# State-space scan and bilinear feed-forward: C of the later blocks loaded by head pairs and turned by VectorE

## The chip, the core and the metric

One NeuronCore of a Trainium2 chip runs the whole program. The metric is the device time of one execution in microseconds (us); the time before is the median of three runs. TensorE (PE) does the matrix products, its weight loads are listed as PEld; VectorE (DVE), ScalarE (ACT) and GpSimd (POOL) do elementwise work; SyncE (SP) issues most DMAs, GpSimd and ScalarE some.

## What is computed

Two stages. The first is a chunked linear recurrence over 4 x 8 sequences (batch x heads) of 768 tokens, with a state of 16 x 32 per sequence; the second is a feed-forward layer `(x Wa) * (x Wb) Wo` over the 3072 tokens, with 256 inputs and 1536 hidden columns. Cut to what matters:

```python
for c in range(nc):                       # chunks of 32 tokens
    L = np.exp(cum[..., :, None] - cum[..., None, :]) * causal
    CB = np.einsum('bhin,bhjn->bhij', Cc, Bc)
    y_intra = np.einsum('bhij,bhjd->bhid', CB * L, xc)
    y_inter = np.einsum('bhin,bhnd->bhid', Cc, state) * np.exp(cum)[..., None]
    y[:, :, sl] = y_intra + y_inter
    Bx = np.einsum('bhjn,bhjd->bhjnd', Bc, xc) * decay_from_j[..., None, None]
    state = decay_full[..., None, None] * state + np.sum(Bx, axis=2)
x = y.transpose(0, 2, 1, 3).reshape(3072, 256)
out = ((x @ w_a) * (x @ w_b)) @ w_out
```

## The kernel before

**Tiling.** The scan runs in 6 blocks of 128 tokens (not 32). A block of one pair of batches is a unit of work called a pair: pair p is block p // 2 and batches 2 (p % 2) and the next, so there are 12 pairs, two to a block. The decay factors are multiplied into B and C beforehand: C by the running product of `a` over its value in the middle of the block, B by the reciprocal of that (`fCl`, `fBl` for pairs 4 to 11; `late_rows`, `late_factors` and `fb` make them, on GpSimd and VectorE).

**One pair of 4 to 11**, step by step:
1. `loads_bc`, `loads_x`: SP issues the DMAs of C, B and x (tokens on the partitions; each run of 16 floats of B or C is 64 bytes).
2. `prep`: GpSimd scales C and B to f16, one 128x256 instruction each (`scale_bc`, L316), and x (`scale_x`, L305).
3. `transposes`: TensorE turns two 128x128 tiles of B and two of C, against the identity (L342), into a bank of PSUM; ScalarE copies B out twice, masked by the parity of the head (L346), and C once (L355).
4. `scores` (L372): 16 small products C B^T into four PSUM banks `SC`.
5. `mask`: the causal mask on the four fourths of the scores. VectorE does a fourth in one instruction (L426). Of pairs 4 to 8 the last fourth goes to GpSimd instead: ScalarE copies it out of PSUM (L423), GpSimd multiplies (L424).
6. Per block, `group`: `outputs` (L522 state part, L432 scores times x, L461 the sums for the next state), the evacuation to `XB` (ScalarE L555, VectorE L557), and on VectorE the state sums (L579).

**The feed-forward** of block k follows: 12 units (`bunit`, L693: two products into PSUM banks of the first and of the second weight matrix; ScalarE copies the first out, L639; VectorE multiplies, L703), then four output tiles (`bout`, L718), copied out by ScalarE (L730) and stored by SP (L731). For pairs 0 to 3 the units are per pair (`unit`, L615, L639, L646; `out_half`, L661, L673).

**Order.** The schedule is written out by hand: each engine takes its instructions in program order, and so does each DMA queue. What waits, holds up what stands behind it on its engine. Four PSUM banks (`ff0` to `ff3`) rotate for units, output tiles and transposes, in the order that the digits of `BANKS` give. Around the change, TensorE's order is: `group(2)`, transposes of pair 6, an output half, transposes of pair 7, another output half, scores of pair 6, units; the same with `group(3)` and pairs 8 and 9; from there on, pair by pair.

**Queues.** At the start GpSimd's queue loads the weights `Wa`, `Wb`, `Wo`, pair 1's and pair 2's inputs. SP loads pair 0's and, after the first half of `Wo` has landed, pair 3's (L851, L854, L855), then pairs 4, 5 and so on. Stores of outputs stand behind all of these loads on SP.

Of the kernel before, what the change touches and what calls it, by code (L numbers as in the profile page):

```python
# [10 lines left out]
f32 = mybir.dt.float32  # L11
# [8 lines left out]
YS = 16.0  # L20

BANKS = (
    "1301302130213023120312031023120312031203210230123012302103210320132013210231023103201231"
    "0231023102301320132013201321032103210321032103210321032130213021302130213021302130213021"
    "3021302"
)


# [1 line left out]
def kernel(  # L30
# [13 lines left out]
    nc = tc.nc  # L44
# [44 lines left out]
    Wo = big.tile([128, NK, d_model], f16, name="Wo")  # L89
    X2T = big.tile([128, P0, 2, 2, Q], f16, name="X2T")  # L90
    XB = big.tile([128, NBLK - P0 // NBP, 2, 2, NBP, Q], f16, name="XB")
    U32 = big.tile([128, NP, 2, 2 * D], f32, name="U32")
    gU = big.tile([128, NP, 2, 2 * D], f32, name="gU")
    maskbd = big.tile([128, H, D], f16, name="maskbd")
    warm = big.tile([128, 128], f16, name="warm")
    causal_q = big.tile([128, Q], f16, name="causal_q")
# [8 lines left out]
    Ps = big.tile([BH, NL, Q], f32, name="Ps")  # L105
    fBl = big.tile([128, NL, NBP * 2 * H], f32, name="fBl")
    fCl = big.tile([128, NL, NBP * 2 * H], f32, name="fCl")
    hr = big.tile([BH, NG], f32, name="hr")
    hs = big.tile([BH, NG], f32, name="hs")
    hsx = big.tile([128, nb, NG], f32, name="hsx")  # L110
# [22 lines left out]
    def bank(name):  # L133
        return psf.tile([128, 512], f32, name=name, tag=f"ff{next(banks)}")


    def tiles(p):
        Bn = inp.tile([128, H, 2, N], f32, name="bn", tag="bn")
        Cn = inp.tile([128, H, 2, N], f32, name="cn", tag="cn")
        Xn = inp.tile([128, H, 2, D], f32, name="xn", tag="xn")  # L140
        pair_in[p] = (Bn, Cn, Xn)

# [16 lines left out]
    def load2(eng, p, which):  # L159
        if p < P0:  # L160
            return [load1(eng, p, which, bt) for bt in range(2)]
        blk, bp = divmod(p, NBP)
        return eng.dma_start(
            by_token(pair_in[p][which]).rearrange("p t h n -> p (t h) n"),
            (B, C, x)[which][2 * bp : 2 * bp + 2, :, blk * Q : (blk + 1) * Q, :].rearrange("t h q n -> q (t h) n"),
        )

    def load_w(W, t, f=None):
        src = (moe_w_a if W is Wa else moe_w_b).rearrange("(f p) e -> p f e", p=128)[:, :, t * KC : (t + 1) * KC]
# [30 lines left out]
    nc.vector.memset(hsx, 0.0)  # L200
    nc.vector.memset(causal_q, 1.0)
    nc.vector.memset(c32, 0.0)
    x1 = load1(nc.sync, 1, 2, 0)
    nc.sync.dma_start(c32[0:BH], p32_t.ap())
    nc.gpsimd.affine_select(
# [70 lines left out]
    def late_rows(eng):  # L276
        k0 = P0 // NBP
        eng.tensor_tensor(
            out=Ps, in0=Pr[:, k0:], in1=rmid[:, k0:].unsqueeze(2).broadcast_to((BH, NL, Q)), op=ALU.mult
        )  # L280

    def late_factors():
        for c0 in range(0, Q, 32):
            nc.vector.transpose(fCl[c0 : c0 + 32], Ps[:, :, c0 : c0 + 32])

    st = {}
    stores = []
# [19 lines left out]
    def scale_bc(p, which, eng, factor=None):  # L307
        blk, bp = divmod(p, NBP)
        name = ("bm", "cm")[which]
        if p >= P0:  # L310
            f = (fBl, fCl)[which][:, blk - P0 // NBP].rearrange("p (b t h) -> p b t h", b=NBP, t=2)[:, bp]
        else:
            f = (f_c(blk) if which else fB[:, blk])[:, :, bp]
        raw = by_token(pair_in[p][which]) if p >= P0 else pair_in[p][which].rearrange("p h r n -> p r h n")
        m_ = pre.tile([128, 2, H, N], f16, name=name, tag=name)
        eng.tensor_tensor(  # L316
            out=m_,
            in0=raw,
            in1=(f if factor is None else factor).unsqueeze(3).broadcast_to((128, 2, H, N)),
            op=ALU.mult,  # L320
        )
        st.setdefault(p, {})[name] = m_
    def transposes(p, ps=None, between=None, apart=False):
        s = st[p]
        if p >= P0:
            ps = [bank("tr").bitcast(f16)] * 2
            TB, TC = ps[0][:, 0:256], ps[0][:, 256:512]
            on_dve = False
        elif ps is None:
            ps = [bank("tb") if p == 1 else SC[0], SC[1]] if apart else None  # L330
            on_dve = apart
            TB, TC = (TT[:, 0:256], TT[:, 256:512]) if ps is None else [t_.bitcast(f16)[:, 0:256] for t_ in ps]
        else:
            on_dve = True
            TB, TC = [t_.bitcast(f16)[:, 0:256] for t_ in ps]
        BT = mid.tile([128, 2, 2, 2, 64], f16, name="bt", tag="bt")
        CT = mid.tile([128, 2, Q], f16, name="ct", tag="ct")
        b_ = []

        def turn(T_, src):  # L340
            for r in range(2):
                nc.tensor.transpose(T_[:, r * 128 : (r + 1) * 128], src[:, r].rearrange("p h n -> p (h n)"), ident)  # L342

        def copy_bt(e):
            o_ = BT[:, e].rearrange("p r t i -> p (r t i)")
            b_.append(nc.scalar.activation(out=o_, in_=TB, func=AF.Copy, scale=par[:, e : e + 1]))  # L346

        turn(TB, s["bm"])
        if between:
            between()  # L350
        turn(TC, s["cm"])
        copy_bt(0)
        copy_bt(1)
        if p >= P0:
            nc.scalar.copy(CT.rearrange("p t q -> p (t q)"), TC)  # L355
            s["BT"], s["CT"] = BT.rearrange("p e r t i -> p e r (t i)"), CT
            return
        c_ = (nc.vector.tensor_copy if on_dve else nc.scalar.copy)(
            CT.rearrange("p t (i r) -> p r (t i)", r=2), TC.rearrange("p (r c) -> p r c", r=2)
        )  # L360
        if apart:
            for i_ in b_:
                tc.declare_no_dep(c_.ins, i_.ins.name, reason="reads of two banks")
        s["BT"], s["CT"] = BT, CT

# [205 lines left out]
    def state_sums(p, bts=(0, 1)):  # L571
        blk, bp = divmod(p, NBP)
        for bt in bts:
            g = G[:, 2 * bp + bt, blk : blk + 1]
            ds = st[p]["DS"][bt]
            if blk == 0:
                nc.vector.tensor_scalar(U32[:, p, bt], ds, g, None, ALU.mult)
            else:
                nc.vector.scalar_tensor_tensor(  # L579
                    out=U32[:, p, bt], in0=ds, scalar=g, op0=ALU.mult, in1=gU[:, p, bt], op1=ALU.add  # L580
                )

    def state_spread(p):
# [16 lines left out]
            )  # L600
        if blk + 1 < NG:
            nc.gpsimd.tensor_tensor(
                out=gU[:, p + NBP],
                in0=U32[:, p],
                in1=G[:, 2 * bp : 2 * bp + 2, blk + 1].unsqueeze(2).broadcast_to((128, 2, 2 * D)),
                op=ALU.mult,
            )
# [125 lines left out]
    def loads_bc(p, eng=None):  # L733
        if p < NP:
            tiles(p)
            for w in (1, 0):
                load2(eng or nc.sync, p, w)

    def loads_x(p, eng=None):
        if p < NP:  # L740
# [73 lines left out]
    for w in range(2):  # L814
        for bt in range(2):
            load1(nc.gpsimd, 2, w, bt)
    wo0 = load_wo(0)
    for bt in range(2):
        load1(nc.gpsimd, 2, 2, bt)
# [61 lines left out]
        out_mm(c // 2, c % 2, o[c], range(6))  # L881
    scale_bc(3, 0, nc.gpsimd)
    scale_bc(3, 1, nc.gpsimd)
    late_rows(nc.gpsimd)
    scale_x(3, nc.gpsimd)
    pull(2)
    pv(2)
    for c in range(3):
        out_mm(c // 2, c % 2, o[c], range(6, NK))
        out_store(c // 2, c % 2, o[c])  # L890
    state_sums(2)
    h = unit(2, 0, lambda: transposes(3, apart=True))
    h()
    late_factors()
    fb(2)
    h = unit(2, 1)

    def prep(p, spread=()):
        if p < NP:
            scale_bc(p, 1, nc.gpsimd)  # L900
            scale_bc(p, 0, nc.gpsimd)
        for q in spread:
            if q // NBP < NBLK - 1:
                state_spread(q)
# [33 lines left out]
        return [lambda k=k: bunit(blk, k) for k in ks]  # L938

    scores(3)  # L940
    prep(4, (2,))
    loads_x(4, nc.sync)
    for p in range(6, NP):
        loads_bc(p)
        if p < 10:
            loads_x(p - 1, nc.sync)
    mask(product(3, 3), by_pool=True)
    mask(product(3, 0))
    h()
    for m in range(1, 3):  # L950
# [3 lines left out]
    go((2, 2), (2, 3), (2, 4))  # L954
    pull(3)
    pv(3)
    go((2, 5))
    transposes(4)
    state_sums(3)
# [23 lines left out]
    h()  # L983
    go((3, 5))
    group(2)
    transposes(6)
    out_half(3, 0)
    transposes(7)
# [7 lines left out]
    scale_x(6, nc.scalar)  # L996
    bgo(2, 3, 4)
    stage(7, True)
    fb(5)
    prep(8)  # L1000
    prep(9)
    prep_x(8)
# [2 lines left out]
        loads_x(p)  # L1005
    masked(7, (0, 1, 2), *bu(2, 5, 6, 7, 8, 9, 10, 11))
    group(3)
    transposes(8)
    bout(2, 0)
    transposes(9)  # L1010
# [6 lines left out]
    masked(8, (2,), *bu(3, 0, 1, 2, 3, 4, 5))  # L1017
    for blk in range(4, NBLK):
        pB = blk * NBP + 1
        stage(pB, False)  # L1020
        if blk + 1 < NBLK:
            transposes(pB + 1)
        if blk > 4:
            prep_x(pB)
        masked(pB, (0, 1))
        bout(blk - 2, 2)
        masked(pB, (2, 3), *bu(blk - 1, 6, 7, 8, 9))
        group(blk)
        bout(blk - 2, 3)
        bgo(blk - 1, 10, 11)  # L1030
        if blk + 1 < NBLK:
            stage(pB + 1, False, (pB - 1, pB))
            prep_x(pB + 1)
            masked(pB + 1, (0, 1))
            bout(blk - 1, 0)
            masked(pB + 1, (2,))
            transposes(pB + 2)
            bout(blk - 1, 1)
            masked(pB + 1, (3,), *bu(blk, 0, 1, 2, 3, 4, 5))
    last = NBLK - 1  # L1040
    bout(last - 1, 0)
    bout(last - 1, 1)
# [37 lines left out]
```

## Time and profile before

| | us |
|---|---|
| runs: median of 3 (lowest to highest) | 124.99 (124.78 to 125.30) |
| the profiled execution, its own time | 125.11 |
| its span, first to last instruction | 123.40 |
| TensorE busy | 117.3 |
| VectorE / ScalarE / GpSimd busy | 91.0 / 75.7 / 61.2 |

The span is what the views show; the 1.71 us beside it are the same run's start and end. Busy time of TensorE counts overlapping, pipelined instructions, so it says little about how tightly they follow; the chain of work that ended last says more. It is followed back from the last instruction: at each step to what released it, or to the instruction before it on its engine. In a row of a timeline come start, length, engine, line, operation, what it writes and reads, how often, and in brackets how long the engine had been idle and what released it. In a row of a group come the count, the busy time, the mean duration in ns and the idle time before. Busy time by stage, in us:

| stretch (us) | PE | DVE | ACT | POOL | DMA share |
|---|---|---|---|---|---|
| 13 to 24 | 10.60 | 9.02 | 7.44 | 8.26 | full |
| 24 to 31.5 | 7.50 | 4.46 | 4.66 | 6.27 | 0.77 |
| 31.5 to 39.5 | 8.00 | 6.92 | 5.70 | 4.56 | 0.94 |
| 39.5 to 51 | 11.48 | 10.06 | 8.78 | 8.04 | 0.99 |
| 51 to 63 | 11.96 | 10.80 | 8.93 | 9.78 | 0.86 |
| 63 to 78 | 15.00 | 12.71 | 11.02 | 9.20 | 0.41 |
| 78 to 96 | 18.00 | 15.48 | 10.32 | 3.73 | 0.09 |

### The profile page before, as it was taken

To read this page: it belongs to the slowest core of one execution; us is meant where nothing else is said; L and a number is where in the kernel's file an instruction comes from. 1 tells how busy PE (TensorE), PEld (TensorE's weight loads), DVE (VectorE), ACT (ScalarE), POOL (GpSimd) and SP (SyncE) were. 2 spreads that over 40 slices of the span, in tenths; PEclk is the share of its full clock that TensorE was granted. 3 is DMA by queue.
4 is the path that set the end of the run, shared out by engine and by line. 5 is a ranking of instruction groups with operands and counts; after the bars stand their busy time and mean duration, and the time that the engine had idled before them with its cause. 6 is when DMAs were issued, how large, how long until landed. Compare 5 with 4: busy or idle time off the path is not lost.

```text
span 123.4 us, 3704 instructions
## 1 busy us (share of the span) xinstructions
PE 117.3 (95%) x1456; PEld 80.0 (65%) x1456; DVE 91.0 (74%) x182; ACT 75.7 (61%) x158; POOL 61.2 (50%) x88
## 2 busy tenths in 40 slices
PE   6799799999999999999999999999999999999990
PEld 2345669889898798744477465757464775555890
DVE  3999598973995979799986988996889544747200
ACT  0447846837669866987669767457637746657220
POOL 7997989099492994097996970056000000000000
PEclk9999999999999999999999999999999999999999
DMA  3999999978899989799977601011101012010122
GB/s 66 195 155 210 185 198 204 164 137 77 89 125 115 108 111 103 91 118 93 129 271 169 204 5 45 5 43 45 43 0 43 5 43 88 0 48 0 43 85 85
DMA packets 56401, 12.15 MB, mean 99 GB/s; under 512 B 51168, under 2 KB 55936, under 8 KB 56384
## 3 DMA queue, kind: packets, MB, share of 16 engines
q1 hardware_dynamic: 51808, 7.43, 36.3%
q0 software_dynamic: 2304, 4.06, 17.4%
q10 hardware_dynamic: 2272, 0.43, 1.8%
q8 instruction: 11, 0.18, 0.6%
q14 instruction: 6, 0.05, 0.1%
HBM read 11.13 MB, written 3.15 MB: 116 GB/s over the span
## 4 chain that ended last, share of the span: by engine, by line
PE 85%; DMA 7%; DVE 5%; issue 1%; ACT 0%; DVEq 0%
PE ops L718 17%; PE aps L693 17%; PE bps L693 16%; PE ops L661 9%; PE aps L615 8%; PE bps L615 7%; DMA Wb<-in_moe_w_b_dram 5%; PE SC L372 2%; PE SC L432 2%; PE tr L342 2%; DMA a_sb<-in_a_dram 2%; DVE hk L646 1%; PE bps L628 1%; PE SC L447 1%; PE SC L522 1%; DVE fC L246 1%
## 5 line engine op out<-in xcount | busy, mean ns | idle before, releaser
L639 ACT COPY asb<-aps 128x512 f32<-128x512 f32 x72 | 41.9, 587 | 16.0 <-PE aps L693 10.4
L703 DVE TENSOR_TENSOR hkb<-bps,asb 128x512 f16<-128x512 f32 x48 | 32.3, 688 | 11.8 <-ACT asb L639 10.4
L693 PE MATMUL aps<-XB,Wa 128*128 128x512 f16 x96 | 28.6, 379 | 0.0
L693 PE MATMUL bps<-XB,Wb 128*128 128x512 f16 x96 | 28.5, 379 | 0.0
L718 PE MATMUL ops<-Wo,hkb 128*128 128x256 f16 (+1 forms) x204 | 22.8, 267 | 0.0
L718 PEld LDWEIGHTS <-hkb 128*128 128x128 f16 x204 | 18.4, 98 | 3.0
L426 DVE TENSOR_TENSOR t<-SC,causal_q 128x512 f16<-128x512 f32 x27 | 17.3, 681 | 2.2 <-PE SC L372 2.2
L646 DVE TENSOR_TENSOR hk<-bps,asb 128x512 f16<-128x512 f32 x24 | 15.6, 681 | 3.5 <-ACT asb L639 2.1
L693 PEld LDWEIGHTS <-Wb 128*128 128x128 f16 x96 | 9.9, 103 | 11.0 <-issue 0.2
L693 PEld LDWEIGHTS <-Wa 128*128 128x128 f16 x96 | 9.7, 104 | 9.2 <-issue 0.3
L730 ACT ACTIVATE osb<-ops 128x256 f32<-128x256 f32 (+1 forms) x16 | 6.0, 376 | 12.7 <-PE ops L718 12.6
L615 PE MATMUL bps<-X2T,Wb 128*128 128x256 f16 x84 | 12.6, 273 | 0.1
L615 PE MATMUL aps<-X2T,Wa 128*128 128x256 f16 x84 | 12.5, 273 | 0.2 <-DVE hk L646 0.2
L305 POOL TENSOR_SCALAR x<-xn 128x512 f16<-128x512 f32 x8 | 11.9, 1489 | 0.7
L661 PE MATMUL ops<-Wo,hk 128*128 128x256 f16 x96 | 11.7, 273 | 0.0
L661 PEld LDWEIGHTS <-hk 128*128 128x128 f16 x96 | 9.0, 98 | 1.2
L615 PEld LDWEIGHTS <-Wb 128*128 128x128 f16 x84 | 8.5, 103 | 1.1 <-issue 0.5
L615 PEld LDWEIGHTS <-Wa 128*128 128x128 f16 x84 | 8.4, 104 | 1.2 <-issue 0.5
L424 POOL TENSOR_TENSOR t<-tmp,causal_q 128x512 f16<-128x512 f32 x5 | 5.8, 1156 | 6.2 <-ACT tmp L423 6.1
L426 DVE TENSOR_TENSOR t<-SC,causal 128x512 f16<-128x512 f32 x13 | 8.2, 678 | 0.3 <-PE SC L387 0.2
L595 POOL TENSOR_TENSOR spair<-U,ch 128x128 f16<-128x128 f32 x8 | 3.1, 398 | 10.3 <-DVE U L579 10.3
L346 ACT ACTIVATE bt<-tr,ch 128x256 f16<-128x256 f16 x16 | 6.7, 472 | 0.5 <-PE tr L342 0.5
(101 smaller groups left out, 136.1 us busy)
## 6 DMA issues: line engine op xcount, KB each, us to landing
out_dram<-osb SPq DMA_DIRECT2D x23, 128.0 KB, 1.8
xn<-in_x_dram SPq DMA_DIRECT2D x5, 256.0 KB, 4.6
cn<-in_C_dram SPq DMA_DIRECT2D x8, 128.0 KB, 4.3
bn<-in_B_dram SPq DMA_DIRECT2D x8, 128.0 KB, 4.7
Wo<-in_moe_w_out_dram POOLq DMA_DIRECT2D x2, 384.0 KB, 5.9
xn<-in_x_dram POOLq DMA_DIRECT2D x3, 256.0 KB, 4.8
Wa<-in_moe_w_a_dram POOLq DMA_DIRECT2D x2, 192.0 KB, 5.5
xn<-in_x_dram SPq DMA_DIRECT2D x3, 128.0 KB, 3.5
```

Of the source, the lines that this page charges most:

```text
L305: eng.tensor_scalar(xo, xi, XS, None, ALU.mult)
L346: b_.append(nc.scalar.activation(out=o_, in_=TB, func=AF.Copy, scale=par[:, e : e + 1]))
L424: nc.gpsimd.tensor_tensor(out=o_, in0=tmp, in1=c_, op=ALU.mult)
L426: nc.vector.tensor_tensor(out=o_, in0=i_, in1=c_, op=ALU.mult)
L615: nc.tensor.matmul(ps[:, kk * 2 * Q : (kk + 1) * 2 * Q], w_up(W, k, f), X2T[:, p, :, f], start=(f == 0), stop=(f == 1), skip_group_check=True,
L639: (nc.vector.tensor_copy if on_dve else nc.scalar.copy)(asb, a_ps)
L646: nc.vector.tensor_tensor(out=s["hk"][:, 2 * k2 : 2 * k2 + 2, :].rearrange("p k q -> p (k q)"), in0=b_ps, in1=asb, op=ALU.mult)
L661: nc.tensor.matmul(o_ps[:, 0:d_model], hk[:, k, bt * Q : (bt + 1) * Q], Wo[:, k, :], start=(k == 0), stop=(k == NK - 1), skip_group_check= ...
L693: nc.tensor.matmul(t_, w_up(W, k, f), XB[:, blk - P0 // NBP, f].rearrange("p t j q -> p (t j q)"), start=(f == 0), stop=(f == 1), skip_gro ...
L703: return lambda: nc.vector.tensor_tensor(out=s["hk"][:, k], in0=ps[1], in1=asb, op=ALU.mult)
L718: nc.tensor.matmul(o_ps[:, 0:w], hk[:, k, c * Q : (c + 1) * Q], Wo[:, k, cs], start=(k == 0), stop=(k == NK - 1), skip_group_check=True,)
L730: nc.scalar.activation(out=o_sb[:, 0:w], in_=o_ps[:, 0:w], func=AF.Copy, scale=1.0 / (YS * YS))
```

## The change

C of blocks 2 to 5 (pairs 4 to 11), and B of block 5 (pairs 10 and 11), take another way to the layout with heads and state on the partitions:

- **Load.** A whole block comes at once: for each of the four head pairs m and each head e of it, one DMA into 32 partitions, four neighbouring tokens (256 bytes) to a run; 8 DMAs of 32 KB for both pairs of the block (`load_block`).
- **Factors.** They are needed in this layout: `spread_rows` copies rows of `Ps` to `Pq` in 16 DMAs on SP, `block_factors` turns `Pq` on VectorE into `fCq`; `last_factors` takes the reciprocal for B of block 5, in place of `fb(5)`. `late_rows`, which computes `Ps` on GpSimd, moves ahead of the loads of `Wo`; `late_factors` and `fb(2)` move ahead of `pv(2)`.
- **Scale and turn.** GpSimd scales the block in one 128x512 instruction (`scale_block`), VectorE turns it in 32x32 blocks in one 128x512 instruction (`turn_block`), SBUF to SBUF. The transposes on TensorE and ScalarE's copy of C go; of B of block 5 the transposes go too, and ScalarE's two masked copies read SBUF.
- **Masks.** The last fourth of pairs 9, 10 and 11 goes by ScalarE and GpSimd.

`BANKS` is written anew (two banks less are taken), the number of buffers of B, C and the states changes, and `mask(product(3, 3), by_pool=True)` moves ahead of `prep(4)`.

```diff
+    def by_block(blk, which):
+        return blk >= P0 // NBP and (which == 1 or blk == NBLK - 1)
...
+    def load_block(eng, blk, which):
+        raw = inp.tile([128, nb, 2, 4, N], f32, name="rq", tag="rq", bufs=3)
+        st[("raw", blk, which)] = raw
+        for m, e in itertools.product(range(4), range(2)):
+            eng.dma_start(
+                raw[32 * m : 32 * m + 32, :, e].rearrange("i b g n -> i b (g n)"),
+                (B, C)[which][:, 2 * m + e, blk * Q : (blk + 1) * Q, :].rearrange("b (i g) n -> i b (g n)", g=4),
+            )
+
+    def scale_block(blk, which, eng):
+        f = fCq[:, blk - P0 // NBP, :, 0 : 2 * nb] if which else fBq
+        m_ = pre.tile([128, 4, nb, 2, N], f16, name="mq", tag="mq", bufs=2)
+        eng.tensor_tensor(
+            out=m_.rearrange("p g b e n -> p (b e) g n"),
+            in0=st[("raw", blk, which)].rearrange("p b e g n -> p (b e) g n"),
+            in1=f.rearrange("p g j -> p j g").unsqueeze(3).broadcast_to((128, 2 * nb, 4, N)),
+            op=ALU.mult,
+        )
+        st[("scaled", blk, which)] = m_
+
+    def turn_block(blk, which):
+        t_ = mid.tile([128, nb, Q], f16, name="tq", tag="tq", bufs=3)
+        nc.vector.transpose(
+            t_.rearrange("p b (i g) -> p g b i", g=4),
+            st[("scaled", blk, which)].rearrange("p g b e n -> p g b (e n)"),
+        )
+        st[("turned", blk, which)] = t_
...
+    nc.vector.memset(Pq, 0.0)
...
+    def last_factors():
+        nc.vector.reciprocal(fBq, fCq[:, NL - 1, :, 0 : 2 * nb])
...
+    def spread_rows(eng):
+        for m, b in itertools.product(range(4), range(nb)):
+            eng.dma_start(Pq[32 * m + 2 * b : 32 * m + 2 * b + 2], Ps[b * H + 2 * m : b * H + 2 * m + 2])
+
+    def block_factors():
+        nc.vector.transpose(
+            fCq.rearrange("p k g j -> p (k g) j"), Pq.rearrange("p k (i g) -> p k g i", g=4)
+        )
...
         if p >= P0:
-            ps = [bank("tr").bitcast(f16)] * 2
-            TB, TC = ps[0][:, 0:256], ps[0][:, 256:512]
-            on_dve = False
+            if by_block(blk, 0):
+                TB = st[("turned", blk, 0)][:, 2 * bp : 2 * bp + 2].rearrange("p t q -> p (t q)")
+            else:
+                TB = bank("tr").bitcast(f16)[:, 0:256]
...
-        turn(TB, s["bm"])
+        if not by_block(blk, 0):
+            turn(TB, s["bm"])
...
-        turn(TC, s["cm"])
+        if p < P0:
+            turn(TC, s["cm"])
...
-            nc.scalar.copy(CT.rearrange("p t q -> p (t q)"), TC)
+            s["CT"] = st[("turned", blk, 1)][:, 2 * bp : 2 * bp + 2]
...
     for w in range(2):
         for bt in range(2):
             load1(nc.gpsimd, 2, w, bt)
+    late_rows(nc.gpsimd)
+    spread_rows(nc.sync)
     wo0 = load_wo(0)
...
-    late_rows(nc.gpsimd)
     scale_x(3, nc.gpsimd)
+    late_factors()
+    fb(2)
     pull(2)
     pv(2)
...
     state_sums(2)
+    block_factors()
     h = unit(2, 0, lambda: transposes(3, apart=True))
     h()
-    late_factors()
-    fb(2)
...
     pv(3)
+    turn_block(2, 1)
     go((2, 5))
...
     group(2)
+    turn_block(3, 1)
     transposes(6)
...
-    fb(5)
+    last_factors()
...
     group(3)
+    turn_block(4, 1)
     transposes(8)
...
     for blk in range(4, NBLK):
         pB = blk * NBP + 1
-        stage(pB, False)
-        if blk + 1 < NBLK:
-            transposes(pB + 1)
+        stage(pB, True)
...
         masked(pB, (0, 1))
+        if blk + 1 < NBLK:
+            turn_block(blk + 1, 0)
         bout(blk - 2, 2)
-        masked(pB, (2, 3), *bu(blk - 1, 6, 7, 8, 9))
+        masked(pB, (2,), *bu(blk - 1, 6, 7))
+        if blk + 1 < NBLK:
+            turn_block(blk + 1, 1)
+        bgo(blk - 1, 8, 9)
+        if blk + 1 < NBLK:
+            transposes(pB + 1)
         group(blk)
...
-            stage(pB + 1, False, (pB - 1, pB))
+            stage(pB + 1, True, (pB - 1, pB))
...
-            masked(pB + 1, (3,), *bu(blk, 0, 1, 2, 3, 4, 5))
+            bgo(blk, 0, 1, 2, 3, 4, 5)
```

## The prediction

> **What bounds the kernel now.** I read the page first: busy shares, slices, and the chain that ended last.
>
> ```profile
> span 123.4 us, 3704 instructions
> ...
> PE 117.3 (95%) x1456; PEld 80.0 (65%) x1456; DVE 91.0 (74%) x182; ACT 75.7 (61%) x158; POOL 61.2 (50%) x88
> ...
> PEclk9999999999999999999999999999999999999999
> ...
> PE 85%; DMA 7%; DVE 5%; issue 1%; ACT 0%; DVEq 0%
> ```
>
> TensorE carries 85% of the chain, at full granted clock. The other engines matter only where TensorE waits for them. Next I read the chain in order of time. From 17 us on its pieces follow each other with hardly a gap; this is the turn from block 3's scan to pair 8's scores:
>
> ```profile
> 62.96 0.56 PE SC L432 x32
> 63.64 0.33 PE tr L342 x4
> 63.97 1.31 PE ops L718 x12
> 65.50 1.31 PE ops L718 x12
> 66.81 0.33 PE SC L372 x16
> ```
>
> The first output half ends at 63.97 + 1.31 = 65.28, the second starts at 65.50; pair 9's four transposes lie between: 0.22 us, 55 ns each. A transpose lasts longer than that (the group rows give 219 to 221 ns), but four overlap and only the pitch costs chain time. So work taken off TensorE is worth its pitch, unless something else arrives later than TensorE does.
>
> Third, VectorE's timeline over the same stretch:
>
> ```profile
> 63.84 0.47 DVE L579 SCALAR_TENSOR_TENSOR U<-SC,G,gU 128x64 f32<-128x64 f32 x2 [0.21 <-PE SC L461]
> ...
> 64.33 1.39 DVE L557 TENSOR_SCALAR XB<-SC 64x512 f16<-64x512 f32 x2
> ...
> 65.75 0.47 DVE L579 SCALAR_TENSOR_TENSOR U<-SC,G,gU 128x64 f32<-128x64 f32 x2
> ...
> 67.18 1.89 DVE L426 TENSOR_TENSOR t<-SC,causal_q 128x512 f16<-128x512 f32 x3 [0.96 <-PE SC L372]
> ```
>
> VectorE works without a pause to 66.22 and idles 0.96 us until the scores come. Last, the groups by shape, the SP queue's timeline and the issue times of two stores:
>
> ```profile
> L246 DVE STREAM_TRANSPOSE fC<-Pe 32x64 f32<-32x64 f32 x4 | 0.9, 235 | 0.1
> ...
> L284 DVE STREAM_TRANSPOSE fCl<-Ps 32x128 f32<-32x128 f32 x4 | 1.2, 299 | 0.0
> ```
> ```profile
> 21.63 1.28 SPq L154 DMA_DIRECT2D bn<-in_B_dram  x2
> 22.95 1.36 SPq L154 DMA_DIRECT2D cn<-in_C_dram  x2
> 24.36 1.31 SPq L154 DMA_DIRECT2D xn<-in_x_dram  x2
> ```
> ```profile
> L731 SPq DMA_DIRECT2D out_dram<-osb x16: 332/332/333, 65.7 to 120.2; - x16
> L675 SPq DMA_DIRECT2D out_dram<-osb x8: 383/406/1278, 59.3 to 63.7; - x8
> ```
>
> Two more shapes of elements give VectorE's turn: 64 more elements cost 64 ns. And an issue on SP costs 0.33 us alone, 0.41 beside other traffic.
>
> **The change, part by part** (against the profiled execution: 125.11 us, span 123.40, 1.71 around it; the median of the runs is 124.99, 0.12 lower).
>
> TensorE transposes. Pairs 4 to 9 lose C's two, 12 in all; pairs 10 and 11 lose all four, 8 in all. 20 x 55 ns = **-1.10 us** on the chain. One page speaks of far more: the Trainium skill (TensorE: Matmul & The Clock Gate, Part 4: PE-mode transpose) gives about 275 ns for one in a kernel, 5.5 us for 20 by that; the pitch in the rows decides against it.
>
> The turns. Five of 128x512 f16. From the two rows, 299 + 384 x 1.0 = 0.69 us each. No row shows f16: two elements at a time would make it 163 + 256 = 0.42, strided writes at half rate 1.2. I take 0.69, as both rows cost one element per ns.
> Each must end before its block's scores:
> - Block 4 (pair 8). It is put behind group(3), on an engine busy to 66.22: it ends at 66.93, and scores follow some 0.05 us later (ScalarE's copy at 50.72 + 0.38 = 51.10, scores at 51.15). TensorE, 0.22 us shorter over this stretch, arrives at 66.59: a new wait of 0.40. Behind the scores stand the six units of block 3.
> - Block 3 (pair 6), the same place: VectorE's sums end at 50.64, the turn at 51.35, scores at 51.41, TensorE there at 51.22 - 0.22 = 51.00: 0.41. Behind it the reciprocal fb(4) (0.35) still fits before the masks.
> - Block 2 (pair 4): VectorE is idle 0.82 us before 37.97, scores come at 39.46: nothing.
> - Block 5, C and B: between pair 9's masks and units. VectorE is behind TensorE there; with 2 x 0.69 added and one mask (0.68) gone it ends the state sums at 81.7 instead of 81.47, TensorE reaches pair 10's scores at 82.06 - 0.22 = 81.84. Nothing, with 0.1 to spare.
> So **+0.81 us**; with 0.42 a turn 0.27, with 1.2 some 2.2 (0.5 more on each of the two, and 0.4 on pair 10's).
>
> block_factors, a turn of 128x512 f32 (0.70), late_factors (1.24) and fb(2) (0.34): VectorE waits 1.48 us before the state sums at 28.31 and 1.51 before 30.29; the first two fill the former to 28.4, the other the latter. Nothing; in exchange the 1.6 us at 31.4 go, where VectorE wasn't last. The memset of Pq, 512 elements, by the rows 20 elements 75 ns and 148 elements 182 ns about 0.5 us, lies in the 1.19 us wait for `a` before 2.98. Nothing.
>
> ScalarE loses 8 copies of C (0.38) and gains 3 mask copies (0.59): 1.3 us less, no bound. GpSimd's 3 masks (1.16) fall behind 73 us, where it idles (8.07 us before 81.45). VectorE loses 3 x 0.68 there. Nothing on the chain.
>
> GpSimd's scaling: 10 x 0.62 out, 5 of twice the size in; the nearest rows for 512 elements are 1.16 (mask) and 1.49 (scaling x). Near equal in sum, but the first of a block comes all at once: x of pair 5, ready at 46.60 now, slips 0.6 us to some 47.0 (47.3 by the dearer row), needed at 47.4. Nothing, bound +0.2.
>
> The queues at the start. late_rows (1.03) now runs on GpSimd at 15.7, before the first half of Wo, both x loads of pair 2 and the second half. The 0.48 us that GpSimd waits at 18.30 absorb half, so pair 2's B and C are scaled 0.55 later, at 20.8, before the transposes at 21.35; x lands by 24.7 for ScalarE's 24.52. The pair 3 loads on SP wait for Wo, which lands at 22.6 for 21.6. Before them SP now issues 16 small spread copies. With 0.40 + 0.05 us gap each: from 16.7 to **23.9**, so pair 3's loads start 2.3 us late. C's last load (issued 23.63, landing 2.6 later) must be there 0.62 + 0.06 before the transposes at 29.93: slack 3.0. Bounds: 0.33 + 0.04 (22.6, no loss) to 0.62 + 0.05 (the 64 KB loads beside the weights: 27.4, so 5.8 - 3.0 = 2.8 us of TensorE waiting). I take nothing, as the stores are nearer in packets (128 and fewer) than those loads (512).
> Then each block of C is 8 issues, 3.6 us, for two of 1.3 to 1.6; but its 1024 packets of 256 B replace 4096 of 64 B, so the DMA engines, eight or nine tenths busy to 60 us on the page, clear sooner. B of pair 5 leaves SP at 33 us instead of 31.7 and is due scaled at 38.96; with 4.8 to 5.1 us to land (rows of B) that is 38.7. No loss, and no slack.
>
> Sum: -1.10 + 0.81 = **-0.29**, 124.82 for the profiled execution, **124.7** for the median.
>
> **The rivals.**
> (1) *The turns hide.* If a turn takes 0.42, the waits are 0.14 each: -0.8, 124.2; with none, 123.9. For it: VectorE's 0.96 us of idle before the masks. Against it: that idle is as long as TensorE's way to the scores, and the turn must end before them.
> (2) *SP's queue decides: slower.* The 16 spread copies and eightfold block loads hold up pair 3's inputs; TensorE stands at the transposes near 30 us, with all units behind it. It decides from a pitch of 0.50 us. At 0.58 SP is free at 26.0, 4.4 - 3.0 = +1.4, and the second row of eight adds 1.0 to pair 5's B, part of which the first wait covers: about 126.1; at 0.67, 127.5. For it: loads beside the weights took 0.60 to 0.69. Against: 406 ns for stores of 128 packets. The rule speaks for it: the Trainium skill (DMA: Bandwidth & Descriptors, Rules for kernel authors) says of many small transfers that one should coalesce, as under 64 KB "you're paying mostly overhead"; the 0.33 us row for a store of 128 packets agrees that a floor exists.
> (3) *Transposes cost their full length*, 0.22 us each: 20 x 0.22 - 0.81 = -3.6, 121.4. Against: the 0.22 us that hold four of them. The page named above would have it so.
> (4) *The turn costs 1.2:* +1.1 net, 126.1.
>
> **How the numbers follow.** Forecast 0.46 (124.2 to 125.3 by itself), (1) 0.29, (2) 0.19, (3) 0.01, (4) 0.05. 0.5% is 0.62 us, about what can be told from no change: faster below 124.37, slower above 125.61. Faster: all of (3), 0.26 of (1), 0.08 of the forecast (waits half as long): 0.35. Slower: 0.16 of (2), (4): 0.21. Same: 0.44. The range takes (1) in whole, and (2) to a pitch of 0.55: 123.8 to 125.9.
>
> **What would show it.** L342 with 28 transposes instead of 48 at the same pitch. Five f16 stream transposes of 0.69 us. Scores of pairs 6 and 8 released by VectorE's turn after 0.4 us of idle TensorE, those of pairs 4 and 10 not. SP's 16 spread copies ending before 24.5, pair 3's transposes released without a wait. I am wrong if the turn is released earlier than the scores (then 123.9), or if TensorE idles near 30 or 38 us (then above 125).

## The result: slower by 5.3%, and the profile after

| | before | after |
|---|---|---|
| median of 6 runs (lowest to highest), us | 124.88 (124.55 to 125.30) | 131.44 (130.97 to 132.13) |
| the profiled execution: its own time, span | 125.11, 123.4 | 132.13, 130.4 |

The ratio is 1.0533, its 95% interval 1.0491 to 1.0575. The forecast was 124.7, in a range to 125.9. First the page of the changed kernel: span, busy time by engine, the granted clock in 40 slices, the chain of waits by engine.

```profile
span 130.4 us, 3723 instructions
...
PE 119.2 (91%) x1436; PEld 79.9 (61%) x1436; DVE 97.2 (75%) x186; ACT 75.5 (58%) x153; POOL 64.3 (49%) x86
...
PEclk9999999999999999689999999999999999999999
...
PE 51%; SPq 17%; DVE 10%; DMA 9%; POOL 5%; issue 4%; ACT 2%; DVEq 0%; POOLq 0%
```

TensorE's share of the chain falls from 85% to 51%. SP's queue, which wasn't in the list before, now holds 17%, VectorE 10% instead of 5%, and two slices have a clock below 0.9. TensorE's busy time grows by 1.9 us only (119.2 against 117.3), so most of the 7.0 us of span are waits, and the queue is the first to ask. SP's timeline after (start, length, line, what it writes and reads, how often):

```profile
16.90 9.96 SPq L329 DMA_DIRECT2D Pq<-Ps  x16
26.97 1.38 SPq L163 DMA_DIRECT2D bn<-in_B_dram  x2
...
46.14 1.45 SPq L172 DMA_DIRECT2D xn<-in_x_dram  x1
```

The 16 spread copies take 0.62 us apiece with their gaps. Pair 3's B is issued at 26.97 instead of 21.63. TensorE's timeline after, the four rows with the waits that matter (in brackets the idle time before, and who ended it):

```profile
31.04 0.29 PE L395 MATMUL SC<-ident,bm 128*128 128x128 f16 x2 [0.61 <-POOL bm L366]
32.45 0.29 PE L395 MATMUL SC<-ident,cm 128*128 128x128 f16 x2 [1.13 <-POOL cm L366]
...
52.25 0.41 PE L487 MATMUL SC<-t,x 128*32 128x128 f16 x16 [1.92 <-POOL x L355]
...
73.66 0.41 PE L427 MATMUL SC<-tq,bt 32*128 32x128 f16 x16 [0.91 <-DVE tq L199]
```

The first two are pair 3's B and C, late from SP. The third is x of pair 5: SP issues it at 46.14 (last row above) instead of 36.62, behind the queue's 5.3 us of delay and behind the eight issues of two blocks of C. The fourth is the turn of block 4. What follows the 1.92 us shows in the busy time by stretch (stretch; length and busy time of PE, PEld, DVE, ACT, POOL with instructions; granted clock; DMA share; GB/s):

```profile
49.00:52.20 3.20, 1.32 (x39) 0.83 (x37) 1.75 (x3) 0.69 (x2) 2.99 (x3) 1.00 1.11 147
52.20:55.40 3.20, 3.15 (x48) 2.40 (x49) 2.37 (x7) 1.33 (x3) 0.62 (x1) 0.61 0.40 75
55.40:58.70 3.30, 3.30 (x36) 2.15 (x35) 2.23 (x4) 2.36 (x6) 0.20 (x1) 0.86 0.48 69
```

Behind the idle time the mean granted clock is 0.61 and then 0.86; in finer stretches it stands at 0.50 from about 53.0 to 56.3. The groups by shape after give the turn and C's transposes (count; busy time, mean ns; idle before):

```profile
L199 DVE STREAM_TRANSPOSE tq<-mq 128x512 f16<-128x512 f16 x5 | 6.6, 1315 | 0.0
...
L395 PE MATMUL SC<-ident,cm 128*128 128x128 f16 x6 | 0.8, 222 | 1.2 <-POOL cm L366 1.1
```

Of C's transposes those of pairs 0 to 3 remain (six in this row, two in another), as the change says; and a turn takes 1.31 us. How late TensorE starts certain steps, from the timelines (us; the last three columns are kernels of the experiments below):

| TensorE starts | before | after | after - before | no copies | rows by TensorE | pairs as words |
|---|---|---|---|---|---|---|
| transposes of pair 2 | 21.35 | 21.74 | +0.39 | 21.97 | 21.79 | 21.50 |
| scores of pair 3 | 31.50 | 33.98 | +2.48 | 32.12 | 31.94 | 31.65 |
| group of block 2 | 47.05 | 49.67 | +2.62 | 47.30 | 47.12 | 46.80 |
| transposes of pair 6 | 47.98 | 52.70 | +4.72 | 48.97 | 48.24 | 47.82 |
| scores of pair 6 | 51.15 | 57.32 | +6.17 | 52.89 | 52.16 | 50.87 |
| scores of pair 8 | 66.74 | 73.66 | +6.92 | 69.23 | 68.50 | 66.34 |
| scores of pair 11 | 90.45 | 97.37 | +6.92 | 92.94 | 92.22 | 89.62 |

Read down the fourth column, the loss has four steps: 2.1 at pair 3's inputs, 2.1 at x of pair 5, 1.45 between the transposes and the scores of pair 6 (the low clock), 0.75 at block 4's turn; 0.4 stand before pair 2. These 1.45 are of this execution (see the clock, below). From pair 8 on nothing is lost, and nothing gained: the pitch of eight transposes is gone there, but TensorE comes to pair 10's scores 9.80 us after pair 9's, against 9.59 before and 9.38 with pairs as words. VectorE has two turns of 1.31 us in that stretch, and TensorE's next unit waits 0.18 us for VectorE.

### The profile page after: what moved, and what is told of

It is laid out like the page before. It is cut to its first block, busy times and chain, and to the rows that moved or that the text cites. A ratio compares the mean times of both kernels' runs of the same rounds, so it can differ in the third digit from the quotient of the medians.

```text
span 130.4 us, 3723 instructions
## 1 busy us (share of the span) xinstructions
PE 119.2 (91%) x1436; PEld 79.9 (61%) x1436; DVE 97.2 (75%) x186; ACT 75.5 (58%) x153; POOL 64.3 (49%) x86
## 4 chain that ended last, share of the span: by engine, by line
PE 51%; SPq 17%; DVE 10%; DMA 9%; POOL 5%; issue 4%; ACT 2%; DVEq 0%; POOLq 0%
PE aps L748 15%; PE bps L748 14%; PE ops L773 13%; SPq L181 7%; DMA Pq<-Ps 4%; SPq L329 4%; DVE t L481 4%; SPq L172 3%; DMA xn<-in_x_dram 3%; PE ops L716 3%; SPq L163 3%; DMA a_sb<-in_a_dram 2%; PE SC L487 2%; PE SC L427 1%; DVE tq L199 1%
## 5 line engine op out<-in xcount | busy, mean ns | idle before, releaser
L479 POOL TENSOR_TENSOR t<-tmp,causal_q 128x512 f16<-128x512 f32 x8 | 9.3, 1161 | 17.7 <-ACT tmp L478 17.5
L481 DVE TENSOR_TENSOR t<-SC,causal_q 128x512 f16<-128x512 f32 x24 | 15.3, 681 | 2.4 <-PE SC L427 2.4
L716 PE MATMUL ops<-Wo,hk 128*128 128x256 f16 x96 | 13.3, 296 | 0.0
L716 PEld LDWEIGHTS <-hk 128*128 128x128 f16 x96 | 9.8, 106 | 1.9
L478 ACT COPY tmp<-SC 128x512 f32<-128x512 f32 x11 | 6.5, 586 | 3.2 <-PE SC L427 2.2
L199 DVE STREAM_TRANSPOSE tq<-mq 128x512 f16<-128x512 f16 x5 | 6.6, 1315 | 0.0
```

What stands on the lines that cost most here:

```text
L199: nc.vector.transpose(t_.rearrange("p b (i g) -> p g b i", g=4), st[("scaled", blk, which)].rearrange("p g b e n -> p g b (e n)"),)
L479: nc.gpsimd.tensor_tensor(out=o_, in0=tmp, in1=c_, op=ALU.mult)
L481: nc.vector.tensor_tensor(out=o_, in0=i_, in1=c_, op=ALU.mult)
L716: nc.tensor.matmul(o_ps[:, 0:d_model], hk[:, k, bt * Q : (bt + 1) * Q], Wo[:, k, :], start=(k == 0), stop=(k == NK - 1), skip_group_check= ...
```

## The experiments

**1. No copies.** Is it the queue? The 16 spread copies go; `Pq` is filled with a constant, so the factors on C of blocks 2 to 5 and B of block 5 are left out.

```diff
-    nc.vector.memset(Pq, 0.0)
+    nc.vector.memset(Pq, 1.0e-3)
...
-    spread_rows(nc.sync)
```

> The changed kernel without the 16 copies from Ps to Pq: Pq is filled with 0.001 instead, so C of pairs 4 to 11 and B of pairs 10 and 11 carry a constant in place of their decay factors. Queue theory (SP's queue, 16 x 0.60 us late from 27 us on, holds up pair 3's inputs and x of pair 5): SP starts pair 3's loads at 22.6 instead of 27.0, the waits of TensorE near 31 (about 2.1 us), at block 2's products (2.1) and the lower clock behind it (1.4) go: 126.3 to 127.2 us. Turn theory (the 1.31 us turns and VectorE carry most of the 6.6 us): 129.5 or more.

127.36 (ratio 1.0202, 1.0184 to 1.0221), 0.2 above the expected range: 4.1 of the 6.6 us come back, and with them the waits at pair 3, the low clock and most of the wait for x of pair 5 (0.55 left). TensorE's timeline of this kernel keeps what the queue doesn't explain:

```profile
52.89 0.40 PE L427 MATMUL SC<-tq,bt 32*128 32x128 f16 x16 [0.91 <-DVE tq L199]
...
69.23 0.41 PE L427 MATMUL SC<-tq,bt 32*128 32x128 f16 x16 [0.91 <-DVE tq L199]
```

The scores of pairs 6 and 8 wait 0.91 us for a turn, each. In the changed kernel only the second is seen: at the low clock TensorE comes to the scores of pair 6 later than the turn.

**2. The copies alone.** The other way round: the kernel before, with `late_rows` early and the 16 copies, whose result nobody reads.

```diff
+    late_rows(nc.gpsimd)
+    spread_rows(nc.sync)
     wo0 = load_wo(0)
...
-    late_rows(nc.gpsimd)
     scale_x(3, nc.gpsimd)
```

> The kernel before, with nothing of the change but late_rows ahead of Wo's loads and the 16 copies from Ps to Pq on SP; nothing reads Pq. Queue theory: pair 3's loads start at 27 us instead of 21.6, TensorE waits some 2 us near 30 us, 0.4 more from late_rows on GpSimd: 127.0 to 128.0 us. Turn theory (the copies are hidden): 124.7 to 125.4.

129.50 (1.0319, 1.0242 to 1.0395), more than expected. TensorE's timeline of this kernel, and below it the granted clock from its page:

```profile
31.58 0.29 PE L347 MATMUL SC<-ident,bm 128*128 128x128 f16 x2 [1.91 <-POOL bm L321]
32.94 0.29 PE L347 MATMUL SC<-ident,cm 128*128 128x128 f16 x2 [1.07 <-POOL cm L321]
...
33.83 1.06 PE L620 MATMUL aps<-X2T,Wa 128*128 128x256 f16 x4
```
```profile
PEclk9999999999679999999999999999999999999999
```

The copies alone cost 1.91 + 1.07 of waiting at pair 3, and then four products take 1.06 instead of 0.60 us, at a low clock. That clock is the part that wasn't expected: three of the four executions had a mean clock of 0.987 and took 129.41 to 129.75; the fourth, at 1.0, took 127.68, within the expected range. Runs 1 and 2 together show the cause of the larger part: the copies, with nothing else of the change but the earlier `late_rows`, cost 4.6 in the median and 2.8 in the execution at full clock; without them the change costs 2.5.

**3. Prices.** What an issue and a turn cost by themselves: probes at the end of the kernel before, on scratch (its time says nothing).

```diff
+    nc.sync.dma_start(sb[16:32], sa[16:32])
...
+        nc.vector.transpose(hb, ha)
+        nc.vector.transpose(
+            hb.rearrange("p (b i g) -> p g b i", b=4, g=4), ha.rearrange("p (g b i) -> p g b i", g=4, b=4)
+        )
...
```

> The kernel before with probes ahead of its last output tiles, whose time says nothing: copies in SBUF of 2, 2, 8, 16, 32 and 64 rows of 2 KB on SP, and on VectorE twice each the turn of 128x512 f16 in order, with the strided write, with the strided read, 128x256 f16, 128x512 f32 in order and with the strided read, and 32x512 f16. If an issue on SP costs by its packets: 2 rows 0.3 us, less than 64 rows. If few rows cost more: 2 rows 0.56 us, 64 rows 0.33. If the stride makes the turn slow: f16 in order 0.69, strided 1.3.

SP's timeline of this kernel (2, 16 and 64 rows), then its groups:

```profile
116.99 0.62 SPq L1052 DMA_DIRECT2D gU<-gU  x1
...
118.35 0.55 SPq L1054 DMA_DIRECT2D gU<-gU  x1
...
119.57 0.60 SPq L1056 DMA_DIRECT2D gU<-gU  x1
```
```profile
L1059 DVE STREAM_TRANSPOSE X2T<-X2T 128x512 f16<-128x512 f16 x2 | 2.6, 1316 | 0.1
L1067 DVE STREAM_TRANSPOSE gU<-gU 128x512 f32<-128x512 f32 x2 | 2.2, 1080 | 0.1
L1062 DVE STREAM_TRANSPOSE X2T<-X2T 128x512 f16<-128x512 f16 x2 | 1.4, 712 | 0.1
L1066 DVE STREAM_TRANSPOSE gU<-gU 128x512 f32<-128x512 f32 x2 | 1.4, 690 | 2.9 <-DMA gU<-gU 2.9
L1058 DVE STREAM_TRANSPOSE X2T<-X2T 128x512 f16<-128x512 f16 x2 | 1.4, 682 | 0.0
```

A copy within SBUF costs SP 0.55 to 0.64 us (0.78 the first time) whatever its rows, with the traffic of the loads long over: it isn't the neighbours, and it isn't the bytes. Both expectations on SP fail: neither are 2 rows cheap (0.3), nor 64 (0.33). A store to HBM on the same queue costs 0.33. And the turn is 682 ns when it writes in order, 712 when it reads f16 at a pitch of four, but 1316 when it writes f16 at that pitch, which is what `turn_block` does to bring the tokens back into order. For f32 the strided read costs 1080.

**4. The turn in order, the reader strided.** The kernel of run 1, with the turn's output as it falls. TensorE and ScalarE read it in the order of the tokens: four neighbouring tokens lie 128 elements (256 bytes) apart, as the tile's shape gives.

```diff
-        t_ = mid.tile([128, nb, Q], f16, name="tq", tag="tq", bufs=3)
+        t_ = mid.tile([128, 4, nb, 32], f16, name="tq", tag="tq", bufs=3)
...
-            t_.rearrange("p b (i g) -> p g b i", g=4),
+            t_,
...
-        st[("turned", blk, which)] = t_
+        st[("turned", blk, which)] = t_.rearrange("p g b i -> p b i g")
```

> The kernel without the copies, and the turn writes its result in the order in which it reads it; TensorE and ScalarE read it with the stride instead (same factors left out). If the strided f16 write makes the turn 1.31 us: 0.69 us, and the waits before the scores of pairs 6, 8 and 10 shrink by 0.6 each, 1.2 to 1.8 us less than without the copies alone. If an f16 turn of 512 elements takes 1.3 us in any order: no difference, or a loss where TensorE reads with a stride.

131.10 (1.0485, 1.0460 to 1.0509): a miss by 5 us in the wrong direction. Groups of this kernel:

```profile
L429 PE MATMUL SC<-tq,bt 32*128 32x128 f16 x128 | 8.3, 386 | 0.6 <-DVE tq L199 0.6
...
L199 DVE STREAM_TRANSPOSE tq<-mq 128x512 f16<-128x512 f16 x5 | 3.5, 700 | 0.0
```

The turn falls to 700 ns, but the 128 small products of the scores take 8.3 us of TensorE instead of 3.2: a moving operand whose neighbours lie 256 bytes apart costs 386 instead of 216 ns. What it would cost at a pitch of four elements, no run shows.

**5. `late_rows` on VectorE.** In the profile after, VectorE's timeline has a row that took 0.17 us before, and GpSimd's has the moved instruction beside it:

```profile
15.93 0.99 DVE L892 TENSOR_TENSOR hsx<-hs,c 32x20 f32<-32x20 f32 x1
```
```profile
15.79 1.09 POOL L316 TENSOR_TENSOR Ps<-Pr,rmid 32x512 f32<-32x512 f32 x1
```

The small product ends when GpSimd's does, at 16.9. Run 5 is run 1 with `late_rows(nc.vector)`, ahead of those products; the factors are left out as there.

> The kernel without the copies (factors left out as there), with late_rows on VectorE in its idle 1.2 us near 14 us instead of on GpSimd. If late_rows on GpSimd holds VectorE up (its 32x5 product took 1.01 us beside it, 0.14 before) and shifts GpSimd: 0.5 to 0.7 us less than without the copies alone, 126.6 to 126.9 us, transposes of pair 2 at 21.4 instead of 22.0. If that delay is made up later anyway: no difference, 127.2 to 127.5.

126.88 (1.0140, 1.0080 to 1.0200), 0.5 less than run 1, with intervals that overlap; in run 1 a neighbour of that row took 1.01, here all three take 0.14 to 0.17.

**6. Rows spread by TensorE.** The changed kernel without the copies: one f16 product with a 0/1 matrix spreads `Ps` to `Pq`; `late_rows` on VectorE.

```diff
-    spread_rows(nc.sync)
...
+    nc.tensor.matmul(
+        SC[3],
+        sel.rearrange("p m j -> p (m j)"),
+        Ps16.rearrange("p k q -> p (k q)"),
...
+    nc.scalar.copy(Pq.rearrange("p k q -> p (k q)"), SC[3])
```

> The changed kernel, whole, but Pq is made by TensorE: one product of the f16 rows with a 0/1 matrix, placed in TensorE's wait near 16.5 us, instead of the 16 copies; late_rows on VectorE. Queue theory: as without the copies, 126.4 to 127.1 us, 4.3 to 5 less than the changed kernel. If the factors' arrival, not the queue, held things up: the same 131.

126.33 (1.0123, 1.0073 to 1.0173): 5.1 of the 6.6 us are gone. After 17 us TensorE's long waits are 0.90 before the scores of pair 6 and 0.91 before pair 8's, both for the turn.

**7 and 8. The stride on TensorE's output; the loads' order.** Run 7 is run 6 with the turn in order (702 ns) and the order of tokens restored where TensorE writes to PSUM.

```diff
-                SC[m][:, c0 : c0 + Q],
+                SC[m][:, c0 : c0 + Q].rearrange("p (i g) -> p g i", g=4),
```

> As with the rows by TensorE, and the turn writes 32 elements in a row (tokens of a block in the order that the load gives); TensorE reads them in that order and writes its products to PSUM with the stride instead. Turns 0.70 instead of 1.31 us: scores of pairs 6 and 8 wait 0.3 to 0.4 instead of 0.9, block 5's two turns cost half: 1.2 to 2.0 less than with the rows by TensorE alone, 124.8 to 125.5. If TensorE pays for a stride on its output as it did for one on its input: more than with the rows alone.

126.86 (1.0148, 1.0101 to 1.0196): nothing gained that can be told; the intervals overlap, and the profiled executions stand the other way (126.72 against run 6's 126.99). The waits fall to 0.31 and 0.30, but a product takes 301 instead of 216 ns. Run 8 adds to it B ahead of C and x ahead of both on SP, x of pair 5 earlier on GpSimd, and a part of XB's evacuation from VectorE to ScalarE:

> As in order, and: SP loads x of the pair before, then B, then C's block; GpSimd scales B of pair 6 and x of pair 5 ahead of the mask and C of block 3; of the three evacuations of a block VectorE does one and ScalarE two. The turns then end before TensorE arrives at the scores, and x of pair 5 is in time: the 1.1 us of transposes come out nearly whole, 123.6 to 124.4 us. If the load of VectorE or ScalarE, not the place of the turn, sets the wait: 124.8 or more.

126.58 (1.0107, 1.0073 to 1.0142), a miss by 2: the turn's wait goes (scores of pair 8 at 67.32 instead of 67.69), the 0.2 us of strided output for every 16 products stay (0.61 instead of 0.40).

**9. Pairs of tokens as words.** Run 6, with two neighbouring f16 moved as one 4-byte word: 128x256 words, written at a pitch of two words, and C comes out in order. GpSimd scales a block in two instructions.

```diff
-        t_ = mid.tile([128, nb, Q], f16, name="tq", tag="tq", bufs=3)
+        t_ = mid.tile([128, nb, Q // 2], f32, name="tq", tag="tq", bufs=3)
         nc.vector.transpose(
-            t_.rearrange("p b (i g) -> p g b i", g=4),
-            st[("scaled", blk, which)].rearrange("p g b e n -> p g b (e n)"),
+            t_.rearrange("p b (i a) -> p a b i", a=2),
+            st[("scaled", blk, which)].bitcast(f32).rearrange("p a b e n h -> p a b (e n h)"),
```

> The version with the factors spread by TensorE, and the turn moves two neighbouring tokens as one 4-byte word: 128x256 words instead of 128x512 f16 elements, written at a pitch of two words, so C still comes out in the order of the tokens and TensorE reads and writes in a row. GpSimd scales a block in two instructions (about 0.62 each, as its 128x256 rows, against one of 1.10). Theory (what is left against the kernel before is the length of the strided turn, 1.31): 256 words at 0.69 / 2 = 0.35 to 1.08 / 2 = 0.54 plus a little, so 0.4 to 0.6 a turn; TensorE's 0.90 before the scores of pairs 6 and 8 falls to 0.0 to 0.25 each; with the wait before pair 10 that is 1.4 to 2.2 less than 126.33: 124.2 to 125.0, the scores of pair 8 at 66.8 to 67.2. Rival (late loads of block 3 and x of pair 5 on SP set the pace, and the turn only takes up their wait): 126.0 to 126.5, with TensorE waiting for GpSimd's x or B in place of the turn.

124.86 (1.0000, 0.9971 to 1.0028): level with the kernel before. A group of this kernel, and its chain by engine from the page:

```profile
L203 DVE STREAM_TRANSPOSE tq<-mq 128x256 f32<-128x256 f32 x5 | 2.2, 435 | 0.0
```
```profile
PE 90%; DMA 5%; DVE 1%; issue 1%; ACT 0%; POOL 0%; DVEq 0%; POOLq 0%
```

A turn of 435 ns, no wait of TensorE listed after 17 us, and 90% of the chain. GpSimd's two instructions take 1.25 us a block instead of 1.10. The scores of pair 8 come at 66.34, 0.40 ahead of before. From there to pair 11's takes 23.28 us against 23.71: 0.43 less, and in this stretch eight transposes are gone, which at 55 ns are 0.44 (the last mask fourths of pairs 9 to 11 have moved to GpSimd as well).

**10 to 12. Order again.** Run 10 puts two turns earlier on VectorE, run 12 x of pairs 5 to 11 ahead of the blocks (both from run 9); run 11 is the changed kernel, copies and all, with x of pairs 5 to 9 first on SP and x of pair 5 first on GpSimd.

```diff
-        loads_bc(p)
         if p < 10:
             loads_x(p - 1, nc.sync)
+        loads_bc(p)
```

> The version that moves pairs of tokens as words, and two turns earlier in VectorE's order: block 3's between the masks of pair 5, where VectorE idles 0.8 us, block 4's ahead of the state sums of block 3 instead of behind them. Theory (the turn must end before the scores, and what lies idle on VectorE earlier is free): no wait before the scores of pair 6, 0.1 to 0.2 less before pair 8: 0.2 to 0.5 less than the version beside it. Rival (VectorE has no idle time there that TensorE does not need; block 3's C is scaled too late for it): the same or up to 0.5 more, TensorE waiting at the state part of block 2 or at the units of pair 3 for VectorE.

124.84 (0.9980, 0.9950 to 1.0010): no difference that can be told. Its profiled execution is a long one (126.46): no wait for a turn is listed, but TensorE waits 1.24 us for x of pair 5 and 0.89 for a mask by GpSimd near 80 us.

> The version that moves pairs of tokens as words, with the order of the x loads altered: SP issues x of pairs 5 to 9 ahead of the next pair's B and block of C, GpSimd scales x of pair 5 ahead of block 3's C, and GpSimd's own queue issues x of pairs 9 to 11 ahead of scaling block 5's C. Theory (the profile taken of the version without this stood at 124.38 with no wait of TensorE after 16 us, and its other runs were up to 1.5 longer because x came late behind the eight issues of a block, as the version with the early turn shows with 1.24 before x of pair 5): the median comes down to 124.2 to 124.6, and the spread of the runs from 1.5 to under 0.8. Rival (C of block 3 comes late instead, or the spread is of the start): 124.7 to 125.3 with the same spread.

124.84 (1.0005, 0.9974 to 1.0037), runs from 124.33 to 126.27: the median didn't move, and executions of over 125.8 us remain, so the place of x on the queue isn't all that spreads them.

> The changed kernel with one thing altered: SP issues x of pairs 5 to 9 ahead of the next pair's B and block of C, and GpSimd scales x of pair 5 ahead of block 3's C. Theory (the late x of pair 5 leaves TensorE idle for 1.9 us, and the granted clock falls to 0.61 only after so long an idle): no wait for x of pair 5; the wait goes to C of block 3, which lands some 1.2 us later, but is shorter than 1.9; no slice under 0.95 of granted clock; scores of pair 6 at 53.5 to 55.5 instead of 57.3, in all 127.6 to 129.6. Rival 1 (the clock falls from the load of the chip or the loads in flight, not from the idle): a slice near 0.7 in the same place, 130 or more. Rival 2 (the lateness only moves to C of block 3): 130.5 to 132.

130.73 (1.0467, 1.0431 to 1.0503), 1.1 above the expected range; both rivals allow the time. TensorE's timeline of run 11, and the granted clock from its page:

```profile
31.39 0.28 PE L395 MATMUL SC<-ident,bm 128*128 128x128 f16 x2 [1.88 <-POOL bm L366]
32.70 0.28 PE L395 MATMUL SC<-ident,cm 128*128 128x128 f16 x2 [1.01 <-POOL cm L366]
...
55.82 0.40 PE L427 MATMUL SC<-tq,bt 32*128 32x128 f16 x16 [0.75 <-DVE tq L199]
```
```profile
PEclk9999999999679999999999999999999999999999
```

The wait for x of pair 5 is gone, and with it the low clock in that place; but this execution waits 1.88 us at pair 3, and 1.01 right after it, and there the clock falls. So it follows the long idle, not the stage. But the execution of this kernel that took longest, 131.09, had a mean clock of 0.999: a low clock isn't needed for such a time. What x first saves here is partly given back by the 0.75 that the turn now takes in the open.

## Why the prediction was wrong

The step that failed is the pitch of SP's issues: "With 0.40 + 0.05 us gap each: from 16.7 to 23.9", chosen "as the stores are nearer in packets". Measured, it is 0.62 with the gap, and SP is free at 26.9. The bound at 0.62 + 0.05 stood in the text, and rival (2), which decides from 0.50; the choice between the ends was wrong. Run 3 shows why: a copy within SBUF costs 0.55 to 0.64 whether it has 2 or 64 rows, more than a store of 128 rows, so the stores were no fit row, nor could one row of theirs show a floor, as rival (2) has it; the six copies do. Why a copy costs more than a store, no run shows.

- **Rival (2) was the mechanism, and its price too low:** 126.1 at 0.58 and 127.5 at 0.67, where the copies alone come to 129.50 (127.68 at full clock). Its first part was about right: scores of pair 3 are 2.1 later beyond pair 2's lag, for +1.4 (at 0.58) to +2.8 (at 0.67). The second row of eight was priced at 1.0 "part of which the first wait covers". It came as 2.1, at x and not at B of pair 5: pair 3's B is issued 5.3 us late, that x 9.5, as the eight issues of two blocks stand between.
- **The clock was not in the sum at all.** "At full granted clock" was read from before and taken to last. In the profile shown it costs 1.45 between the transposes and scores of pair 6, less what the turn would have made TensorE wait there (0.91 in run 1). It isn't needed for the loss: another execution of the changed kernel, at a mean clock of 1.0, took 131.22. Run 2's executions with and without a low clock differ by 1.7 to 2.1.
- **The turn at 0.69 us** was read from f32 rows that write in order. In order it is 0.68 to 0.70, so the row was good, and the stride, weighed as "strided writes at half rate 1.2", was the case. The places were right: scores of pairs 6 and 8 wait for it, those of pair 4 don't. For 1.2 the text had 0.5 more on each, 0.9; run 1 shows 0.91. It also had 0.4 on pair 10's scores, and these come 0.42 later behind pair 9's than in run 9. `block_factors`, priced 0.70 by the same rows, reads at a pitch of four and took 1.11.
- **`late_rows` at no cost** was wrong by 0.5 at most: GpSimd's own queue was counted, VectorE's small product beside it wasn't.
- **x of pair 5, "bound +0.2"** looked at GpSimd alone. The wait was 1.92 with the late queue, 0.55 without the copies.
- **Right:** 20 transposes are worth their pitch (0.43 measured for eight); the memset (485 ns) and the scaling (1.10 for a block) are hidden. The -0.29 of the forecast can't be told from the 0.0 of run 9, which reaches it only with cheaper turns and without the copies.

What stays open: no version was clearly faster than the kernel before. Run 9's profiled execution has a span 0.7 shorter (122.7 against 123.4), but its runs reach from 124.29 to 127.86, and what spreads them was not found.

## What to carry to other kernels

Count the DMA issues that a change puts on a queue and price them by a row of the same kind (source and destination memory), not of the same size; a queue that runs one transfer late runs late for all behind it, and the next stage pays again. An operation moved off the critical engine has a price that depends on its access pattern: measure it with the pattern that it will have, and ask which side of it (writer, reader, PSUM) takes a stride for least. Here moving pairs as 4-byte words made the turn three times as fast (435 instead of 1315 ns) with no price for TensorE, and 0.15 us a block for GpSimd.

## What the runs showed of the hardware

- A copy within SBUF costs SP 0.55 to 0.64 us for 2 to 64 rows of 2 KB; a store of 128 rows to HBM 0.33.
- Pitch of four elements: f16 write of VectorE's turn 1316 against 682 ns, f16 read 712, f32 read 1080 against 690; TensorE's PSUM output 301 against 216. A moving operand of TensorE whose neighbours lie 256 bytes apart: 386 against 216. The Trainium skill (SBUF — State Buffer, section Door 1: The DMA port swizzle) speaks of lines of 16 bytes in SBUF and 8 in PSUM, of a price for each access to a new line, and of strides of up to 4 elements of f32 or 8 of 16 bits for free. The f16 read (nearly free), the moving operand and the PSUM output agree; the f16 write, at 8 bytes, and the f32 read, at 4 elements, don't.
- The granted clock fell to 0.50 for some 3.4 us in three traces, the probes of run 3 left aside. In the changed kernel it fell 0.7 us after a wait of 1.92 us had ended. In runs 2 and 11 it fell after two waits close together (1.91 and 1.07, 1.88 and 1.01 us); the transposes between them were still at full clock. It didn't fall after 0.61 and 1.13 in the changed kernel, nor after 1.24 in run 10. The Trainium skill (TensorE: Matmul & The Clock Gate, Part 1: The HAM clock gate) puts the fall at an idle window of about 3.4 us; in the changed kernel a shorter one did, and in runs 2 and 11 the two waits with the transposes between them span 3.3 and 3.2.
- A VectorE product of 20 elements took 0.99 instead of 0.17 us while GpSimd multiplied, ending with it. The Trainium skill (SBUF — State Buffer, Who interferes with whom) has it that a VectorE instruction with two SBUF inputs contends with GpSimd's reads; the trace agrees.
